# Transposed last 128 output columns: 72 matmuls of 512 columns in place of 288 of 128, in a gated attention and FFN kernel

## The chip, the cores and the metric

The kernel runs on one core of a Trainium2 chip. The metric is the device time of one execution in microseconds (us).

In the profile PE is TensorE, PEld its loads of the stationary operand ("weights"), DVE VectorE, ACT ScalarE and POOL GpSimd; SP issues transfers, which its queue (SPq) shows.

## The reference, cut to what matters

```python
# x: (1, 2048, 640) bf16; wqkv (640, 1920); wo (640, 640); w_gate, w_up (640, 1728); w_down (1728, 640)
g = sigmoid((x * gate_w).sum(-1, keepdims=True))     # one gate per row
a = linear_attention(x, wqkv, heads=32) @ wo         # (2048, 640)
b = (gelu(x @ w_gate) * (x @ w_up)) @ w_down         # (2048, 640)
return g * a + (1 - g) * b
```

Linear attention is reordered in the kernel so that its output is `pqn @ W2`, with `pqn` (2048 x 640) the normalised queries and `W2` (640 x 640) a small matrix made on the way.

## The kernel before: the parts that matter

One output row tile is 128 rows of 640 columns. The kernel's buffer in PSUM, where TensorE writes its results, is laid out as eight banks of 512 float32. 640 is more than one bank, so each product is made as one matmul of 512 columns and one of 128, both with the same stationary tile: `pqnT` for attention (FA, 5 chunks of the contraction) and `hT` for the FFN (FB, 13 chunks of 128 rows; the last 64 rows are the "half", done in pairs on the two halves of the array).

```python
def FA(i):                                       # attention part of row tile i
    for m in range(KC):                          # KC = 5
        lhs = pqnT[:, m, i * 128:(i + 1) * 128]
        e.matmul(ps[:, b0, :], lhs, w2[:, m, 0:512], ...)
        last = e.matmul(ps[:, b1, 0:128], lhs, w2[:, m, 512:640], ...)
    # ACT: t_sb[i] = g * result
# ... cut ...
def FB(i, main, tail, o):                        # FFN part of row tile i
    pieces = [(ps[:, main, :], 0, 512), (ps[:, tail, o:o + 128], 512, 128)]
    for fc in range(NFC - 1):                    # 13 chunks
        lhs = hT[fc][:, i * 128:(i + 1) * 128]
        for dst, c0, cn in pieces:
            last = e.matmul(dst, lhs, wd[:, fc, c0:c0 + cn], start=False, ...)
    # DVE, per piece: out = (1 - g) * result + t_sb[i]; SP: store.
    # For the very last tile, all 512-column matmuls come first, then its 128-column ones,
    # and each piece is mixed and stored by itself.
```

Earlier stages, whose matmuls are not changed: loads, K and Q projections, M = phi(K)^T x, then the FFN gate and up products with the GELU (71 to 191 us). Five DMA transposes of M feed the product "KV" inside the FFN stage. A row `z` of 640 float32 goes to DRAM, element by element, and comes back as a broadcast.

## Time and profile before

| | before |
|---|---|
| reported time, median of 6 fast runs | 275.88 us (275.61 to 276.31) |
| span of the profiled run | 274.5 us |
| TensorE (PE) busy; granted clock | 98%; 1.0 |
| first attention output matmul | 190.98 us |
| last matmul starts; end | 272.19 us; 274.48 us |

The page of the profile opens with the busy time of each engine (us, share of the span, number of instructions). Its part 4 is the chain of waits followed back from the last instruction.

```profile
span 274.5 us, 4041 instructions
PE 269.6 (98%) x1663; PEld 140.6 (51%) x1696; DVE 138.6 (50%) x234; ACT 78.5 (29%) x133; POOL 26.0 (9%) x28
...
PE 98%; issue 1%; DVE 0%
```

Almost the whole span is one chain of matmuls. The next lines are the timeline where the attention output stage begins: start in us, duration, engine, line, operation, shapes.

```profile
190.98 0.38 PE L754 MATMUL ps<-pool 128*128 128x512 bf16 x1
191.20 0.22 PE L755 MATMUL ps<-pool 128*128 128x128 bf16 x1
191.25 0.38 PE L754 MATMUL ps<-pool 128*128 128x512 bf16 x1
```

Durations overlap (0.38 us long, 0.22 us to the next start), so starts tell the cost. A 512-column matmul holds the stream for about 0.216 us and a 128-column one for about 0.056 us. The chain in order of time gives this more exactly: the two stretches below start 6.79 us apart and hold 25 pairs (a record is missing), 0.2716 us a pair.

```profile
213.69 6.74 PE ps L791 x49
220.48 6.74 PE ps L791 x49
```

The Trainium skill, "TensorE: Matmul & The Clock Gate", section "Wait — 56ns, not 53.3ns?", gives the same two figures, 215.7 and 55.6 ns, as the streamed columns at 2.4 GHz plus about 2.5 ns per matmul. This trace agrees.

Three more lines of the timeline mark instants that are compared later: the first Q matmul, the first FFN matmul and the last matmul.

```profile
8.75 0.38 PE L471 MATMUL ps<-pool 128*128 128x512 bf16 x1
71.36 0.81 PE L646 MATMUL ps<-pool 128*128 128x512 bf16 x3
272.19 0.22 PE L791 MATMUL ps<-pool 128*128 128x128 bf16 x1
```

These lines list the last mixes (DVE) and the last stores (issued by SP), with minimum, median and maximum duration in ns.

```profile
L802 DVE SCALAR_TENSOR_TENSOR pool<-ps,pool x2: 351/551/751, 271.7 to 272.4; 128x512 bf16<-128x512 f32 x1, 128x128 bf16<-128x128 f32 x1
L807 SPq DMA_DIRECT2D out_dram<-pool x2: 333/382/432, 272.5 to 272.9; - x2
```

The mix of 512 columns takes 751 ns. Its store is issued at 272.5 us and occupies SP for 333 ns, so the second and last store follows immediately behind it and takes 432 ns to issue.

### The profile page before, as it was taken

To read this page: it belongs to the slowest core of one execution; us is meant where nothing else is said; L and a number is where in the kernel's file an instruction comes from. 1 tells how busy PE (TensorE), PEld (TensorE's weight loads), DVE (VectorE), ACT (ScalarE), POOL (GpSimd) and SP (SyncE) were. 2 spreads that over 40 slices of the span, in tenths; PEclk is the share of its full clock that TensorE was granted. 3 is DMA by queue.
4 is the path that set the end of the run, shared out by engine and by line. 5 is a ranking of instruction groups with operands and counts; after the bars stand their busy time and mean duration, and the time that the engine had idled before them with its cause. 6 is when DMAs were issued, how large, how long until landed. Compare 5 with 4: busy or idle time off the path is not lost.

```text
span 274.5 us, 4041 instructions
## 1 busy us (share of the span) xinstructions
PE 269.6 (98%) x1663; PEld 140.6 (51%) x1696; DVE 138.6 (50%) x234; ACT 78.5 (29%) x133; POOL 26.0 (9%) x28
## 2 busy tenths in 40 slices
PE   8999999999999999999999999999999999999996
PEld 5555555555545444444444444444555555555553
DVE  1588888410234334999999998635000122212223
ACT  2455555210521453233222232224555100000000
POOL 5000000000000401242332421000000000000000
PEclk9999999999999999999999999999999999999999
DMA  7967999311120211112121121380000010111111
GB/s 226 176 109 121 367 405 380 89 23 27 24 48 22 51 49 50 39 32 48 26 49 33 39 50 25 73 297 14 0 0 2 23 43 32 48 50 48 50 42 54
DMA packets 37104, 22.54 MB, mean 82 GB/s; under 512 B 26463, under 2 KB 35679, under 8 KB 37087
## 3 DMA queue, kind: packets, MB, share of 16 engines
q1 hardware_dynamic: 36213, 21.31, 28.4%
q10 hardware_dynamic: 874, 0.98, 1.0%
q8 instruction: 13, 0.21, 0.3%
q14 instruction: 4, 0.03, 0.0%
HBM read 13.11 MB, written 2.62 MB: 57 GB/s over the span
## 4 chain that ended last, share of the span: by engine, by line
PE 98%; issue 1%; DVE 0%
PE ps L646 41%; PE ps L791 20%; PE ps L456 6%; PE ps L754 6%; PE ps L471 6%; PE ps L553 6%; PE ps L472 2%; PE ps L555 2%; PE ps L755 2%; PE ps L457 2%; PE ps L621 2%; PE ps L420 1%; PE ps L775 1%; PE ps L667 1%; PE ps L685 0%
## 5 line engine op out<-in xcount | busy, mean ns | idle before, releaser
L646 PE MATMUL ps<-pool 128*128 128x512 bf16 x509 | 113.0, 379 | 0.6
L646 PEld LDWEIGHTS ps<-pool 128*128 128x128 bf16 x520 | 50.4, 98 | 59.9
L791 PE MATMUL ps<-pool 128*128 128x128 bf16 (+1 forms) x407 | 56.6, 297 | 0.6 <-issue 0.2
L654 DVE TENSOR_TENSOR pool<-ps,pool 128x512 bf16<-128x512 f32 x52 | 35.7, 687 | 33.4 <-PE ps L646 30.2
L652 ACT ACTIVATE pool<-ps 128x512 f32<-128x512 f32 x52 | 31.0, 597 | 72.4 <-PE ps L646 72.0
L802 DVE SCALAR_TENSOR_TENSOR pool<-ps,pool 128x512 bf16<-128x512 f32 (+1 forms) x32 | 16.2, 547 | 63.8 <-PE ps L791 63.8
L791 PEld LDWEIGHTS ps<-pool 128*128 128x128 bf16 x416 | 31.9, 98 | 25.2 <-issue 1.1
L700 POOL TENSOR_TENSOR pool<-pool 128x640 f32<-128x640 bf16 x16 | 22.4, 1405 | 139.0 <-DMA pool<-z_row 86.5
L481 ACT ACTIVATE pool<-ps 128x640 bf16<-128x640 f32 x32 | 22.4, 704 | 24.0 <-PE ps L457 13.4
L495 DVE SCALAR_TENSOR_TENSOR pool<-ps,pool 128x640 bf16<-128x640 f32 x32 | 26.4, 824 | 2.2
L456 PE MATMUL ps<-pool 128*128 128x512 bf16 x78 | 23.6, 384 | 0.0
L708 DVE TENSOR_TENSOR pool<-pool 128x640 bf16<-128x640 bf16 x16 | 23.1, 1442 | 0.6
L471 PE MATMUL ps<-pool 128*128 128x512 bf16 x76 | 22.7, 379 | 0.1
L754 PE MATMUL ps<-pool 128*128 128x512 bf16 x77 | 21.3, 379 | 0.0
L553 PE MATMUL ps<-pool 128*128 128x512 bf16 x76 | 21.2, 379 | 0.0
L555 PE MATMUL ps<-pool 128*128 128x129 bf16 x80 | 17.6, 220 | 0.2
L472 PE MATMUL ps<-pool 128*128 128x129 bf16 x80 | 17.6, 220 | 0.2
L457 PE MATMUL ps<-pool 128*128 128x128 bf16 x80 | 17.6, 220 | 0.1
L755 PE MATMUL ps<-pool 128*128 128x128 bf16 x80 | 17.5, 219 | 0.2
L759 ACT ACTIVATE pool<-ps,pool 128x640 f32<-128x640 f32 x16 | 12.7, 794 | 9.2 <-PE ps L755 9.2
L491 DVE TENSOR_SCALAR pool<-pool 128x640 bf16<-128x640 bf16 x32 | 10.4, 326 | 5.4 <-ACT pool L481 4.2
L702 DVE TENSOR_REDUCE pool<-pool 128x32 f32<-128x640 f32 x16 | 12.9, 809 | 0.0
(52 smaller groups left out, 125.1 us busy)
## 6 DMA issues: line engine op xcount, KB each, us to landing
out_dram<-pool SPq DMA_DIRECT2D x15, 160.0 KB, 1.8
pool<-in_B_w_gate_dram SPq DMA_DIRECT2D x1, 2080.0 KB, 14.7
pool<-in_B_w_up_dram SPq DMA_DIRECT2D x1, 2080.0 KB, 19.4
pool<-in_A_x_dram SPq DMA_DIRECT2D x1, 1280.0 KB, 10.0
pool<-in_B_w_down_dram SPq DMA_DIRECT2D x1, 1120.0 KB, 5.9
pool<-in_A_x_dram SPq DMA_DIRECT2D x1, 960.0 KB, 5.9
pool<-in_A_wo_dram SPq DMA_DIRECT2D x6, 160.0 KB, 9.5
pool<-in_B_w_down_dram SPq DMA_DIRECT2D x1, 960.0 KB, 8.1
```

Of the source, the lines that this page charges most:

```text
L456: e.matmul(ps[:, b0, :], lhs, wk[:, k, 0:512], start=(k == 0), stop=(k == KC - 1))
L457: last = e.matmul(ps[:, b1, 0:128], lhs, wk[:, k, 512:640], start=(k == 0), stop=(k == KC - 1))
L471: e.matmul(ps[:, b0, :], lhs, wq[:, k, 0:512], start=(k == 0), stop=(k == KC - 1))
L472: last = e.matmul(ps[:, b1, 0:129], lhs, wq[:, k, 512:641], start=(k == 0), stop=(k == KC - 1))
L495: P.op("dve", lambda e: e.scalar_tensor_tensor(dst, ps_flat[:, b0 * 512:b0 * 512 + 640], 1.0 + EPS, e_buf[m], ALU.add, ALU.max), reads=[ba ...
L553: e.matmul(ps[:, bs[n], :], lhs, x_aug[:, i, 0:512], start=(i == 0), stop=(i == NT - 1))
L646: last = e.matmul(ps[:, b, :], w[:, k, fc * 128:(fc + 1) * 128], xT[:, k, j * 512:(j + 1) * 512], start=(k == 0), stop=(k == KC - 1))
L652: P.op("act", lambda e: e.activation(ge[n], ps[:, gb, :], ACT.Gelu_apprx_tanh), reads=[bank[gb]], writes=[r_ge[n]])
L654: P.op("dve", lambda e: e.tensor_tensor(hT[fc][:, j * 512:(j + 1) * 512], ps[:, ub, :], ge[n], ALU.mult), reads=[bank[ub], r_ge[n]], write ...
L708: P.op("dve", lambda e: e.tensor_tensor(pq[i].rearrange("p (h d) -> p h d", h=32), pq[i].rearrange("p (h d) -> p h d", h=32), den[n].unsqu ...
L754: e.matmul(ps[:, b0, :], lhs, w2[:, m, 0:512], start=(m == 0), stop=(m == KC - 1))
L791: last = e.matmul(dst, lhs, wd[:, fc, c0:c0 + cn], start=False, stop=(fc == NFC - 2), skip_group_check=True)
```

## The change

Columns 512 to 639 are now produced transposed: a 128-column slice of `W2` or `w_down` is the stationary tile and 512 rows of `pqnT` or `hT` are streamed past it. The intent is fewer and wider matmuls: 20 in place of 80 for attention, 52 in place of 208 for the FFN. In the transposed layout the gate differs along the free dimension, so the mix needs a broadcast row of 1 - g, which goes through DRAM; the result is turned back by a DMA transpose before it is stored. The half chunk is paired differently, PSUM banks are dealt out anew, and the last row tile is cut 384 + 128.

```diff
@@ (cut: addresses, views, resources; hT[13] half = j % 2 in place of alternate row tiles) @@
+            P.op("sp", lambda e: e.dma_start(omg_dram.rearrange("(i p) -> p i", p=128), omg,
+                                             allow_slow_non_contiguous=True),
+                 reads=[r_omg], writes=[r_od], dma=new_dma_key())
@@ (cut) @@
+                if g == 16:
+                    r_ob = P.sb("omgb", R_OB, R_OB + 2 * S)
+                    dma_in(omg_b, omg_dram.unsqueeze(0).broadcast_to([128, S]), [r_ob], reads=[r_od])
@@ (cut) FA @@
-                        e.matmul(ps[:, b0, :], lhs, w2[:, m, 0:512], start=(m == 0), stop=(m == KC - 1))
-                        last = e.matmul(ps[:, b1, 0:128], lhs, w2[:, m, 512:640],
+                        last = e.matmul(ps[:, b, :], pqnT[:, m, i * 128:(i + 1) * 128], w2[:, m, 0:512],
                                         start=(m == 0), stop=(m == KC - 1))
+            def FA_T(j):
+                    for m in range(KC):
+                        last = e.matmul(ps[:, b, :], w2[:, m, 512:640], pqnT[:, m, j * 512:(j + 1) * 512],
+                                        start=(m == 0), stop=(m == KC - 1))
@@ (cut) FFN @@
+            def FB_T(j, b):
+                    for fc in range(NFC - 1):
+                        last = e.matmul(ps[:, b, :], wd[:, fc, 512:640], hT[fc][:, j * 512:(j + 1) * 512],
+                                        start=False, stop=(fc == NFC - 2), skip_group_check=True)
+                P.op("dve", ... d = ps[:, b, :] - faT[j])
+                P.op("pool", ... d = d * omg_b[:, j * 512:(j + 1) * 512])
+                P.op("pool", ... outT[j] = d + faT[j])
+                P.op("sp", lambda e: e.dma_start_transpose(out_t[j], outT[j]), ...)
+                P.op("sp", ... store out_t[j] to out[0, j * 512:(j + 1) * 512, 512:640])
+            def FB(i, b, extra):
+                pieces = [(b, 0, 512)]
+                if i in extra:                                  # the last row tile
+                    pieces = [(b, 0, 384), (extra[i], 384, 512)]
+                # per piece: matmuls, mix on DVE, store
```

More of the change, by code (lines that the diff above doesn't have):

```diff
@@ L201, in bass_gated_mix__linear_attn_block__geglu_ffn__prompt_kernel @@
     R_T = R_WG
-    assert R_T + NT * 1280 <= R_MT + KC * 640
+    R_FT = R_T + NT * 1024
+    assert R_FT + NSC * 1024 <= R_MT + KC * 640
     R_WO = take(NHC * 640)
     R_W2C = take(NHC * 640)
+    R_OB = R_WO
+    assert R_OB + 2 * S <= R_W2C + NHC * 640
     R_W2 = take(KC * 640)
@@ L219, in bass_gated_mix__linear_attn_block__geglu_ffn__prompt_kernel @@
     TOTAL = off
+    omg_dram = nc.dram_tensor("omg_row", (S,), F32).ap()
     z_dram = nc.dram_tensor("z_row", (640,), F32).ap()
@@ L278, in bass_gated_mix__linear_attn_block__geglu_ffn__prompt_kernel @@
             hT = [v16(R_B + fc * S, S) for fc in range(NFC)]
-            t_sb = [v32(R_T + i * 1280, 640) for i in range(NT)]
-            out_sb = [v16(R_XT + i * 640, 640) for i in range(NT)]
+            t_sb = [v32(R_T + i * 1024, 512) for i in range(NT)]
+            faT = [v32(R_FT + j * 1024, 512) for j in range(NSC)]
+            omg_b = v32(R_OB, S)
+            out_sb = [v16(R_XT + i * 512, 512) for i in range(NT)]
+            outT = [v16(R_XT + NT * 512 + j * 512, 512) for j in range(NSC)]
+            out_t = [v16(R_WV + j * 512, 512).rearrange("p (t d) -> p t d", t=4) for j in range(NSC)]
             e_buf = [v16(R_E + n * 640, 640) for n in range(4)]
@@ L313, in bass_gated_mix__linear_attn_block__geglu_ffn__prompt_kernel @@
             r_mT = [P.sb("mT%d" % c, R_MT, R_MT + KC * 640) for c in range(KC)]
+            r_wo = [P.sb("wo%d" % c, R_WO + c * 640, R_WO + (c + 1) * 640) for c in range(NHC)]
+            r_w2c = [P.sb("w2c%d" % c, R_W2C + c * 640, R_W2C + (c + 1) * 640) for c in range(NHC)]
             r_e = [P.sb("e%d" % n, R_E + n * 640, R_E + (n + 1) * 640) for n in range(4)]
@@ L316, in bass_gated_mix__linear_attn_block__geglu_ffn__prompt_kernel @@
                 _r.fresh = False
-            r_wo = [P.res("wo%d" % c) for c in range(NHC)]
-            r_w2c = [P.res("w2c%d" % c) for c in range(NHC)]
             r_w2 = [P.res("w2_%d" % c) for c in range(NHC)]
@@ L326, in bass_gated_mix__linear_attn_block__geglu_ffn__prompt_kernel @@
             r_zd = P.res("z_dram")
+            r_od = P.res("omg_dram")
             r_den = [P.res("den%d" % n) for n in range(2)]
@@ L626, in G13 @@
                      reads=[bank[b]], writes=[r_ge[n]])
-                for h in range(2):
-                    def half(ap, h=h):
-                        return ap.rearrange("p (t two s) -> p t two s", two=2, s=128)[:, :, h, :]
-                    P.op("dve", lambda e, h=h, half=half: e.tensor_tensor(
-                        half(hT[fc][64 * h:64 * h + 64, j * 512:(j + 1) * 512]), half(ps[64:128, b, :]),
-                        half(ge[n][64:128, :]), ALU.mult),
-                        reads=[bank[b], r_ge[n]], writes=[r_hT[fc][j]])
+                h = j % 2
+                P.op("dve", lambda e: e.tensor_tensor(
+                    hT[fc][64 * h:64 * h + 64, j * 512:(j + 1) * 512], ps[64:128, b, :], ge[n][64:128, :], ALU.mult),
+                    reads=[bank[b], r_ge[n]], writes=[r_hT[fc][j]])
             def G(g):
@@ L734, in bass_gated_mix__linear_attn_block__geglu_ffn__prompt_kernel, with fa_bank @@
                 dma_in(wd[64 * h:64 * h + 64, 13, :], B_w_down[1664:1728, :], [r_wd13[h]])
-            r_t = [P.sb("t%d" % i, R_T + i * 1280, R_T + (i + 1) * 1280) for i in range(NT)]
-            r_out = [P.sb("out%d" % i, R_XT + i * 640, R_XT + (i + 1) * 640) for i in range(NT)]
+            r_t = [P.sb("t%d" % i, R_T + i * 1024, R_T + (i + 1) * 1024) for i in range(NT)]
+            r_fT = [P.sb("fT%d" % j, R_FT + j * 1024, R_FT + (j + 1) * 1024) for j in range(NSC)]
+            r_out = [P.sb("out%d" % i, R_XT + i * 512, R_XT + (i + 1) * 512) for i in range(NT)]
             r_out_b = [P.res("outb%d" % i) for i in range(NT)]
-            out_slot = [0]
-            def next_slot():
-                s = SLOTS[out_slot[0] % 4]
-                out_slot[0] += 1
-                return s
+            r_oT = [P.sb("oT%d" % j, R_XT + NT * 512 + j * 512, R_XT + NT * 512 + (j + 1) * 512)
+                    for j in range(NSC)]
+            r_ot = [P.sb("ot%d" % j, R_WV + j * 512, R_WV + (j + 1) * 512) for j in range(NSC)]
+            fa_ctr = [0]
+            def fa_bank():
+                b = fa_ctr[0] % 8
+                fa_ctr[0] += 1
+                return b
             def FA(i):
-                b0, b1 = next_slot()
+                b = fa_bank()
                 def fn(e):
@@ L752, in fn @@
                     for m in range(KC):
-                        lhs = pqnT[:, m, i * 128:(i + 1) * 128]
-                        e.matmul(ps[:, b0, :], lhs, w2[:, m, 0:512], start=(m == 0), stop=(m == KC - 1))
-                        last = e.matmul(ps[:, b1, 0:128], lhs, w2[:, m, 512:640],
+                        last = e.matmul(ps[:, b, :], pqnT[:, m, i * 128:(i + 1) * 128], w2[:, m, 0:512],
                                         start=(m == 0), stop=(m == KC - 1))
                     return last
-                P.op("pe", fn, reads=[r_pqT[i]] + r_w2, writes=[bank[b0], bank[b1]])
@@ L759, in FA @@
-                P.op("act", lambda e: e.activation(t_sb[i], ps_flat[:, b0 * 512:b0 * 512 + 640], ACT.Copy,
-                                                   scale=gg[:, i:i + 1]),
-                     reads=[bank[b0], bank[b1], r_g], writes=[r_t[i]])
-            def FB_half(i, main, tail):
+                P.op("pe", fn, reads=[r_pqT[i]] + r_w2, writes=[bank[b]])
+                P.op("act", lambda e: e.activation(t_sb[i], ps[:, b, :], ACT.Copy, scale=gg[:, i:i + 1]),
+                     reads=[bank[b], r_g], writes=[r_t[i]])
@@ L767, in fn @@
+            def FA_T(j):
+                b = fa_bank()
                 def fn(e):
                     last = None
-                    for p in range(2):
-                        for c0, cn in ((0, 512), (512, 128)):
-                            for h in range(2):
-                                t = 2 * p + h
-                                r = slice(64 * h, 64 * h + 64)
-                                dst = ps[:, main[t], :] if c0 == 0 else ps[:, tail[h], p * 128:p * 128 + 128]
-                                last = e.matmul(dst, hT[13][r, (i + t) * 128:(i + t + 1) * 128],
-                                                wd[r, 13, c0:c0 + cn], start=(c0 == 0 or p == 0), stop=False,
-                                                skip_group_check=True)
@@ L778, in fn @@
-                    return last
-                P.op("pe", fn, reads=[r_hT[13][i // 4]] + r_wd13, writes=[bank[b] for b in main + tail])
-            def FB(i, main, tail, o):
-                rd = [r_hT[fc][i // 4] for fc in range(NFC - 1)] + r_wd
-                pieces = [(ps[:, main, :], 0, 512), (ps[:, tail, o:o + 128], 512, 128)]
-                def mk(ps_):
-                    def fn(e):
+                    for m in range(KC):
+                        last = e.matmul(ps[:, b, :], w2[:, m, 512:640], pqnT[:, m, j * 512:(j + 1) * 512],
+                                        start=(m == 0), stop=(m == KC - 1))
@@ new lines, in fn, with FB_half @@
+                    return last
+                P.op("pe", fn, reads=r_pqT[4 * j:4 * j + 4] + r_w2, writes=[bank[b]])
+                P.op("act", lambda e: e.activation(faT[j], ps[:, b, :], ACT.Copy),
+                     reads=[bank[b]], writes=[r_fT[j]])
+            def FB_half(j, us, main, tail, extra):
+                def fn(e):
+                    last = None
+                    for u in us:
+                        for h in range(2):
+                            i = 4 * (j + h) + u
+                            r = slice(64 * h, 64 * h + 64)
+                            cuts = [(main[i], 0, 512)]
+                            if i in extra:
+                                cuts = [(main[i], 0, 384), (extra[i], 384, 512)]
+                            for b, c0, c1 in cuts:
+                                last = e.matmul(ps[:, b, 0:c1 - c0], hT[13][r, i * 128:(i + 1) * 128],
+                                                wd[r, 13, c0:c1], start=True, stop=False, skip_group_check=True)
+                    if tail:
+                        for h in range(2):
+                            r = slice(64 * h, 64 * h + 64)
+                            last = e.matmul(ps[:, tail[h], :], wd[r, 13, 512:640],
+                                            hT[13][r, (j + h) * 512:(j + h + 1) * 512],
+                                            start=True, stop=False, skip_group_check=True)
+                    return last
+                P.op("pe", fn, reads=[r_hT[13][j], r_hT[13][j + 1]] + r_wd13,
+                     writes=[bank[main[4 * (j + h) + u]] for u in us for h in range(2)] +
+                     [bank[b] for b in tail] + [bank[b] for b in extra.values()])
@@ new lines, in FB_T, with fn @@
+            def FB_T(j, b):
+                n = j % 2
+                def fn(e):
+                    last = None
+                    for fc in range(NFC - 1):
+                        last = e.matmul(ps[:, b, :], wd[:, fc, 512:640], hT[fc][:, j * 512:(j + 1) * 512],
+                                        start=False, stop=(fc == NFC - 2), skip_group_check=True)
+                    return last
+                P.op("pe", fn, reads=[r_hT[fc][j] for fc in range(NFC - 1)] + r_wd, writes=[bank[b]])
+                d = tmp[n][:, 0:512]
+                P.op("dve", lambda e: e.tensor_tensor(d, ps[:, b, :], faT[j], ALU.subtract),
+                     reads=[bank[b], r_fT[j]], writes=[r_tmp[n]])
+                P.op("pool", lambda e: e.tensor_tensor(d, d, omg_b[:, j * 512:(j + 1) * 512], ALU.mult),
+                     reads=[r_tmp[n], r_ob], writes=[r_tmp[n]])
+                P.op("pool", lambda e: e.tensor_tensor(outT[j], d, faT[j], ALU.add),
+                     reads=[r_tmp[n], r_fT[j]], writes=[r_oT[j]])
+                P.op("sp", lambda e: e.dma_start_transpose(out_t[j], outT[j]),
+                     reads=[r_oT[j]], writes=[r_ot[j]], dma=new_dma_key())
+                P.op("sp", lambda e: e.dma_start(
+                    out[0, j * 512:(j + 1) * 512, 512:640].rearrange("(t p) d -> p t d", p=128), out_t[j]),
+                    reads=[r_ot[j]], dma="out")
@@ L787, in fn @@
+            def FB(i, b, extra):
+                rd = [r_hT[fc][i // 4] for fc in range(NFC - 1)] + r_wd
+                pieces = [(b, 0, 512)]
+                if i in extra:
+                    pieces = [(b, 0, 384), (extra[i], 384, 512)]
+                for n, (pb, c0, c1) in enumerate(pieces):
+                    def fn(e, pb=pb, c0=c0, c1=c1):
                         last = None
                         for fc in range(NFC - 1):
-                            lhs = hT[fc][:, i * 128:(i + 1) * 128]
@@ L790, in fn @@
-                            for dst, c0, cn in ps_:
-                                last = e.matmul(dst, lhs, wd[:, fc, c0:c0 + cn], start=False,
-                                                stop=(fc == NFC - 2), skip_group_check=True)
-                        return last
-                    return fn
-                end = i == NT - 1
-                if not end:
-                    P.op("pe", mk(pieces), reads=rd, writes=[bank[main], bank[tail]])
-                for n, (src, c0, cn) in enumerate(pieces):
-                    b = (main, tail)[n]
-                    if end:
-                        P.op("pe", mk([pieces[n]]), reads=rd, writes=[bank[b]])
-                    P.op("dve", lambda e, src=src, c0=c0, cn=cn: e.scalar_tensor_tensor(
-                        out_sb[i][:, c0:c0 + cn], src, omg[:, i:i + 1], t_sb[i][:, c0:c0 + cn],
-                        ALU.mult, ALU.add),
-                        reads=[bank[b], r_t[i], r_omg], writes=[r_out[i] if n == 0 else r_out_b[i]])
-                    if end:
-                        P.op("sp", lambda e, c0=c0, cn=cn: e.dma_start(
-                            out[0, i * 128:(i + 1) * 128, c0:c0 + cn], out_sb[i][:, c0:c0 + cn]),
-                            reads=[r_out[i] if n == 0 else r_out_b[i]], dma="out")
@@ L810, in FB @@
-                if not end:
-                    P.op("sp", lambda e: e.dma_start(out[0, i * 128:(i + 1) * 128, :], out_sb[i]),
-                         reads=[r_out[i], r_out_b[i]], dma="out")
-            for i in range(NT):
-                FA(i)
-            free = [0, 1, 2, 3, 4, 5, 6, 7]
-            for i in range(0, NT, 4):
-                main, tail = free[0:4], free[4:6]
-                FB_half(i, main, tail)
-                for t in range(4):
-                    FB(i + t, main[t], tail[t % 2], (t // 2) * 128)
-                free = free[6:8] + [main[0], main[1], main[2], tail[0], main[3], tail[1]]
+                            last = e.matmul(ps[:, pb, 0:c1 - c0], hT[fc][:, i * 128:(i + 1) * 128],
+                                            wd[:, fc, c0:c1], start=False, stop=(fc == NFC - 2),
+                                            skip_group_check=True)
@@ new lines, in fn @@
+                        return last
+                    r = (r_out, r_out_b)[n][i]
+                    P.op("pe", fn, reads=rd, writes=[bank[pb]])
+                    P.op("dve", lambda e, pb=pb, c0=c0, c1=c1: e.scalar_tensor_tensor(
+                        out_sb[i][:, c0:c1], ps[:, pb, 0:c1 - c0], omg[:, i:i + 1], t_sb[i][:, c0:c1],
+                        ALU.mult, ALU.add),
+                        reads=[bank[pb], r_t[i], r_omg], writes=[r])
+                    P.op("sp", lambda e, c0=c0, c1=c1: e.dma_start(
+                        out[0, i * 128:(i + 1) * 128, c0:c1], out_sb[i][:, c0:c1]), reads=[r], dma="out")
@@ new lines, in bass_gated_mix__linear_attn_block__geglu_ffn__prompt_kernel @@
+            for j in range(NSC):
+                for i in range(4 * j, 4 * j + 4):
+                    FA(i)
+                FA_T(j)
+            for s_, (m1, tail, m2) in enumerate((((4, 5, 6, 7), (0, 1), (2, 3, 0, 1)),
+                                                 ((4, 5, 6, 7), (2, 3), (0, 1, 2, 3)))):
+                j = 2 * s_
+                for us, ms in (((0, 1), m1), ((2, 3), m2)):
+                    order = [4 * (j + h) + u for u in us for h in range(2)]
+                    main = dict(zip(order, ms))
+                    extra = {NT - 1: 4} if NT - 1 in order else {}
+                    FB_half(j, us, main, tail if us[0] == 0 else (), extra)
+                    if us[0] == 0:
+                        FB_T(j, tail[0])
+                        FB_T(j + 1, tail[1])
+                    for i in order:
+                        FB(i, main[i], extra)
```

## The prediction

> **What bounds the kernel.** TensorE. The page gives PE 98% busy at granted clock 1.0, and the chain of waits is PE for 98% of the 274.5 us span. DVE is at 50%, ACT 29%, POOL 9%. So only what shortens or stalls the matmul stream changes the time.
>
> **What the stream costs now.** In the timeline, 512-column matmuls back to back start every 0.216 us (ten of the FFN group take 2.16). In the output stage a 512 and a 128 column matmul share one stationary tile; 25 such pairs start over 6.79 us (213.69 to 220.48), 0.2716 a pair, so a 128-column one costs 0.0558 us. The weight loads (98 ns each in the groups) are hidden already: no idle time stands at them inside the runs of pairs. The Trainium skill, "TensorE: Matmul & The Clock Gate", section "Wait — 56ns, not 53.3ns?", gives 55.6 and 215.7 ns, with about 2.5 ns fixed per matmul; this trace agrees.
>
> **What the change does on PE.** Columns 512-639 need the same streamed columns either way: attention 80 and FFN 208 matmuls of 128 become 20 and 52 of 512. 288 x 0.0558 = 16.07 us become 72 x 0.2158 = 15.54 us. The gain is 216 fixed costs of 2.5 ns, 0.53 us. The 64-row half chunk (half calls) keeps its paired row halves: 8 pairs of 512 and 8 of 128 become 10 pairs of 512 (the last tile is cut 384 + 128), the same within 0.05 us. Its four entries and exits (two "issue" gaps of about 0.27 us each) remain four. Fewer weight loads free nothing.
>
> **Off the critical path.** ACT: four more copies, each shorter (0.6 us against 0.79), one per 1.08 us of PE. DVE: the mixes lose their 128-wide pieces and gain four subtracts (about 0.69 us). POOL: eight 128x512 operations, about 1.2 us each, estimated from 1.405 us for 128x640. Four DMA transposes (2.6 us to landing) and stores follow; the last some 25 us before the end. Output buffers are not reused, so late stores hold up nobody. The end (128-column piece, mix, 1.6 us store) stays.
>
> **The one real risk.** The gate row goes to DRAM as 2048 four-byte elements, issued at about 52 us on the queue that then carries the five transposes of M (issued 59.8 to 76.9). The similar row of 640 elements took 10.6 us to land. Taking 2 us as fixed, 13.5 ns an element, so 2048 take about 28 us and land at 82 to 84 us. The Trainium skill, "DMA: Bandwidth & Descriptors", section on HWDGE ordering, says that a semaphore increment lands only after every earlier write of that DMA engine; so the transposes may be reported done only then, and PE needs them at 84.5 us (the KV product). No run yet shows it. Probably it just fits; if the transposes move only after the row, PE stalls 1 to 4 us there.
>
> **Prediction.** 275.5 us, range 274.9 to 278.5. Chances: faster by over 2% 0.01, within 2% 0.94, slower by over 2% 0.05.
>
> **What the profile would show.** Attention output stage 20 groups of 1.08 us, about 21.6 us against 21.7; FFN output stage shorter by about 0.4 us; PE still about 98%. The weight-load count falls by 216. The row's landing time is 20 to 35 us; the KV product starts at 84.5 us, or later by the stall.
>
> **What would make it wrong.** The tiny-element write taking over 35 us, or blocking the queue (slower); transposed-output matmuls not running at 0.216 us; a bank wait at the switch of stages; or a hidden weight-load limit in the pairs that I don't see (faster, but by little).

## More of the kernel before

A profile of one execution goes with each kernel; its span is about 1.3 us shorter than the reported time in most executions (1.7 in a few, the profiled one of the kernel before among them: 276.21 us reported, span 274.48).

Runs "in one look" are single executions without a verdict; only their traces are used.

## The result, and the profile after

| | before | after |
|---|---|---|
| reported time, median of 6 fast runs | 275.88 us | 274.82 us (274.61 to 274.97) |
| ratio of fast runs, 95% interval | | 0.9959 (0.9946 to 0.9972) |
| span of the profiled run | 274.476 us | 273.577 us |

A ratio is the mean time of one kernel's fast runs over that of the other's fast runs of the same rounds, so it is not quite the ratio of the medians. The kernel is 0.4% faster, but the gain is 1.06 us by the medians where 0.4 us was predicted (0.53 us less an allowance for a stall), and 274.82 us lies just under the range.

```profile
span 273.6 us, 3628 instructions
PE 269.2 (98%) x1454; PEld 131.4 (48%) x1482; DVE 136.8 (50%) x219; ACT 79.2 (29%) x137; POOL 36.2 (13%) x36
...
PE 96%; DMA 2%; issue 1%; SPq 0%; DVE 0%
```

Weight loads fell by 214. That is exact, counted in the two kernels: 216 fewer in the transposed products, 11 fewer in the half chunk, 13 more because the last tile is cut 384 + 128, which the prediction's sum left out. PE records fell by 209, because some are missing. POOL took on 10 us of work; SP waited for it before the transposes, no matmul did. The 2% of DMA in the chain is a load at the start. The next lines are from the chain in order of time. A transposed attention group (L784) of five matmuls takes 1.08 us, 0.216 us a matmul.

```profile
195.25 1.08 PE ps L784 x5
200.64 1.08 PE ps L784 x5
```

The four instants of the changed kernel are these lines of its timeline: first Q matmul, first FFN matmul, first attention output matmul, last matmul.

```profile
8.53 0.38 PE L481 MATMUL ps<-pool 128*128 128x512 bf16 x1
71.15 1.03 PE L656 MATMUL ps<-pool 128*128 128x512 bf16 x4
190.77 0.81 PE L771 MATMUL ps<-pool 128*128 128x512 bf16 x3
271.45 0.22 PE L849 MATMUL ps<-pool 128*128 128x128 bf16 x1
```

At the end (views of the two source lines of the changed kernel, durations in ns as above) the store before the last is issued earlier (271.6 us, behind a mix of 384 columns that takes 618 ns), and the last store takes 350 ns to issue in place of 432.

```profile
L855 DVE SCALAR_TENSOR_TENSOR pool<-ps,pool x2: 351/484/618, 271.0 to 271.7; 128x384 bf16<-128x384 f32 x1, 128x128 bf16<-128x128 f32 x1
L859 SPq DMA_DIRECT2D out_dram<-pool x2: 333/342/350, 271.6 to 272.1; - x2
```

The single records of the two traces place the difference of the spans, 0.899 us, completely:

| stretch | before | after | gain |
|---|---|---|---|
| start to the first FFN matmul | 71.363 | 71.148 | 0.215 |
| to the first attention output matmul | 119.618 | 119.618 | 0.000 |
| attention output, to the first half chunk | 21.829 | 21.679 | 0.150 |
| FFN output, to the start of the last matmul | 59.380 | 59.007 | 0.373 |
| start of the last matmul to the end | 2.286 | 2.125 | 0.161 |

The two matmul stretches together gain 0.523 us, as the sum of the prediction had it. What it did not have is 0.161 us at the end and 0.215 us at the start. The start's difference is there by the first Q matmul (8.749 against 8.532 us), where the code is the same. The gate row, feared to take 28 us, landed in 10.8. These lines from the list of DMA issues of the changed kernel give a transfer, its size in KB and its time from issue to landing in us.

```profile
omg_row<-pool SPq DMA_DIRECT2D x1, 8.0 KB, 10.8
z_row<-pool SPq DMA_DIRECT2D x1, 2.5 KB, 8.3
```

### The profile page after: what moved, and what is told of

It reads as the page before. It is cut to its first block, busy times and chain, and to the rows that moved or that the text cites. A ratio compares the mean times of both kernels' runs of the same rounds, so it can differ in the third digit from the quotient of the medians.

```text
span 273.6 us, 3628 instructions
## 1 busy us (share of the span) xinstructions
PE 269.2 (98%) x1454; PEld 131.4 (48%) x1482; DVE 136.8 (50%) x219; ACT 79.2 (29%) x137; POOL 36.2 (13%) x36
## 4 chain that ended last, share of the span: by engine, by line
PE 96%; DMA 2%; issue 1%; SPq 0%; DVE 0%
PE ps L656 41%; PE ps L849 16%; PE ps L771 6%; PE ps L481 6%; PE ps L566 6%; PE ps L466 6%; PE ps L823 4%; PE ps L568 2%; PE ps L482 2%; PE ps L467 2%; DMA pool<-in_A_wqkv_dram 2%; PE ps L634 2%; PE ps L784 2%; PE ps L804 1%; PE ps L677 1%
## 5 line engine op out<-in xcount | busy, mean ns | idle before, releaser
L656 PE MATMUL ps<-pool 128*128 128x512 bf16 x509 | 113.0, 379 | 0.6
L656 PEld LDWEIGHTS ps<-pool 128*128 128x128 bf16 x520 | 50.4, 98 | 59.9
L849 PE MATMUL ps<-pool 128*128 128x512 bf16 (+2 forms) x218 | 45.4, 366 | 0.2
L849 PEld LDWEIGHTS ps<-pool 128*128 128x128 bf16 x221 | 21.0, 98 | 24.3 <-issue 0.6
L491 ACT ACTIVATE pool<-ps 128x640 bf16<-128x640 f32 x32 | 22.4, 704 | 23.8 <-PE ps L467 13.4
L855 DVE SCALAR_TENSOR_TENSOR pool<-ps,pool 128x512 bf16<-128x512 f32 (+2 forms) x17 | 12.2, 719 | 33.7 <-PE ps L849 33.6
L466 PE MATMUL ps<-pool 128*128 128x512 bf16 x78 | 23.7, 383 | 0.1
L481 PE MATMUL ps<-pool 128*128 128x512 bf16 x76 | 22.7, 379 | 0.0
L566 PE MATMUL ps<-pool 128*128 128x512 bf16 x76 | 21.2, 379 | 0.0
L828 DVE TENSOR_TENSOR pool<-ps,pool 128x512 f32<-128x512 f32 x4 | 2.8, 692 | 31.0 <-remote 23.9
L771 PE MATMUL ps<-pool 128*128 128x512 bf16 x78 | 17.8, 379 | 0.1
L467 PE MATMUL ps<-pool 128*128 128x128 bf16 x80 | 17.6, 220 | 0.1
L830 POOL TENSOR_TENSOR pool<-pool 128x512 f32<-128x512 f32 x4 | 5.1, 1266 | 75.7 <-DVE pool L828 75.7
L501 DVE TENSOR_SCALAR pool<-pool 128x640 bf16<-128x640 bf16 x32 | 10.4, 326 | 5.2 <-ACT pool L491 3.9
```

The source lines that it names most:

```text
L466: e.matmul(ps[:, b0, :], lhs, wk[:, k, 0:512], start=(k == 0), stop=(k == KC - 1))
L467: last = e.matmul(ps[:, b1, 0:128], lhs, wk[:, k, 512:640], start=(k == 0), stop=(k == KC - 1))
L481: e.matmul(ps[:, b0, :], lhs, wq[:, k, 0:512], start=(k == 0), stop=(k == KC - 1))
L566: e.matmul(ps[:, bs[n], :], lhs, x_aug[:, i, 0:512], start=(i == 0), stop=(i == NT - 1))
L656: last = e.matmul(ps[:, b, :], w[:, k, fc * 128:(fc + 1) * 128], xT[:, k, j * 512:(j + 1) * 512], start=(k == 0), stop=(k == KC - 1))
L771: last = e.matmul(ps[:, b, :], pqnT[:, m, i * 128:(i + 1) * 128], w2[:, m, 0:512], start=(m == 0), stop=(m == KC - 1))
```

## The experiments

Theory: the matmul count is worth 0.52 us, the new end of the kernel another 0.15 us, and the remainder is the scatter of single executions. Rivals: the count is worth more than 2.5 ns a matmul (hidden weight loads), or something systematic in the changed program shortens the start.

In every run the times between the first FFN matmul and the first attention output matmul came out at 119.617 to 119.619 us, so stretches of the trace can be compared to a few ns although reported times scatter by several tenths of a us. From the first Q matmul to the first FFN matmul it was 62.613 to 62.617 us in all 13 profiles, so what differs in the start arises in the first 9.5 us.

### A second look at the kernel before

No edit.

> The kernel before, unchanged, as a second look at it. Only the fixed cost of the matmuls (theory M: 216 fewer at about 2.5 ns, 0.53 us) was predicted to matter, while 1.06 us was measured and 0.90 us stands in the two profiles: 0.52 us in the output stage, 0.215 us before the first FFN matmul (71.363 against 71.148 us) and 0.161 us after the last matmul (2.286 against 2.125 us). Rival N (scatter of single executions): this profile's start of the FFN stage lies anywhere between 71.1 and 71.4 us, its end 2.1 to 2.3 us. Rival S (something systematic, such as the shorter program or the cut of the last tile): the same 71.36 and 2.29 us come again, within 0.05 us. Ratio to before 1.000 +- 0.001 under all.

Measured: 275.68 us, ratio 0.9992 (0.9967 to 1.0017). The first FFN matmul starts at 71.329 us, the matmul stretch is 81.209 us as before, the end 2.279 us (2.286 before). The line below, from the view of one source line, shows its last two stores: minimum, median and maximum duration in ns.

```profile
L807 SPq DMA_DIRECT2D out_dram<-pool x2: 333/382/432, 272.5 to 272.8; - x2
```

The end is systematic: the same 333 and 432 ns came again. The start came again too here, but other runs below moved it by up to 0.94 us. Single executions of this unchanged kernel ranged from 275.22 to 276.26 us, with one more at 277.7 that widened the intervals: 1 us, as large as the gain under study.

### The matmuls cut back to 128 columns

```diff
-    last = e.matmul(ps[:, b, :], w2[:, m, 512:640], pqnT[:, m, j * 512:(j + 1) * 512], ...)
+    for q in range(0, 512, 128):
+        last = e.matmul(ps[:, b, q:q + 128], w2[:, m, 512:640],
+                        pqnT[:, m, j * 512 + q:j * 512 + q + 128], ...)
```

The same was done in the FFN product; everything else is the changed kernel.

> The changed kernel with the transposed products again in matmuls of 128 columns (288 in place of 72, the same streamed columns), all else as changed: the reverse dose of theory M. M expects the stretch from the first attention output matmul to the last matmul, 80.686 us after and 81.209 before, at 81.2 us, the time at 275.3 to 275.4 us, and no idle PE, since a 98 ns weight load per 128 columns was hidden before as well. If the whole 1.06 us came from the matmuls and their weight loads, the time goes to 275.9 us. If the change gained from something else than the number of matmuls, the stretch stays at 80.7 us.

Measured: 275.52 us, ratio to before 0.9985 (0.9963 to 1.0008). Three lines of this run's timeline follow. The first is where the attention output begins and the second shows a transposed group in pieces, 13 starts in 0.67 us (0.89 less the 0.22 of the last one); the third is the last matmul.

```profile
190.86 0.81 PE L771 MATMUL ps<-pool 128*128 128x512 bf16 x3
195.18 0.89 PE L785 MATMUL ps<-pool 128*128 128x128 bf16 x13
272.09 0.22 PE L853 MATMUL ps<-pool 128*128 128x128 bf16 x1
```

The stretch is 272.089 - 190.864 = 81.225 us. It had been 81.209 before and 80.686 after: putting 216 matmuls back costs 0.539 us, 2.5 ns each, and nothing else in the stretch changed. The theory of the count holds, and its rival, a further gain from weight loads saved, falls.

### The matmuls cut to 64 columns

The same edit with 64 in place of 128.

> The changed kernel with the transposed products in matmuls of 64 columns (576 in place of 72). Where does the prediction's 'hidden weight load' end? If only the streamed columns and about 2.5 ns a matmul count, the stretch from the first attention output matmul to the last matmul grows by 504 x 2.5 ns = 1.3 us, to 81.9 us. If a weight load of 128 columns takes as long as some 55 ns of streaming and is exposed as soon as a matmul is shorter, each 64-column one takes about 56 ns, 576 take 32 us in place of 15.5, and the stretch is about 97 us.

Measured in one look: 276.38 us; the stretch is 273.001 - 191.056 = 81.945 us, 1.259 us more than after, exactly 504 x 2.5 ns. In the line below from this run's timeline, 19 matmuls of 64 columns start within 0.53 us (0.72 less 0.19), 29 ns apart.

```profile
195.37 0.72 PE L785 MATMUL ps<-pool 128*128 128x64 bf16 x19
```

The view of that source line shows that each of the 160 attention matmuls had a weight load of its own, 98 ns long:

```profile
L785 PEld LDWEIGHTS ps<-pool x160: 97/98/98, 195.2 to 212.9; 128*128 128x128 bf16 x160
```

Even here the loads are hidden: their records are 98 ns long but, like the matmuls, start 29 ns apart, and loads saved gain nothing. Eight loads in a row bring the same tile here, so this run alone does not show it for a new tile each time. The run with the cut 448 + 64 below does: its last 13 matmuls, of 64 columns, have a tile each, and the 12 loads in this line of that run's timeline start within 0.32 us (0.42 less 0.10), again 29 ns apart.

```profile
271.56 0.42 PEld L849 LDWEIGHTS ps<-pool 128*128 128x128 bf16 x12
```

### The kernel before with the new end (first attempt)

```diff
-    pieces = [(ps[:, main, :], 0, 512), (ps[:, tail, o:o + 128], 512, 128)]
+    pieces = [(ps[:, tail, o:o + 128], 512, 128), (ps[:, main, 0:384], 0, 384),
+              (ps[:, ex, 0:128], 384, 128)]      # last tile only; ex = free[6]
@@ (cut: the same pieces in the half chunk; banks, results and stores per piece) @@
```

> The kernel before with only the end of the changed one: the last tile in pieces of 128, 384 and 128 columns, mixed and stored one by one, so that the last two are as in the changed kernel. Theory E (the end got shorter because the store before the last one is issued earlier, behind a 384-column mix, and is smaller): from the last matmul's start to the end 2.13 us as after, not 2.29 us; the time 275.7 to 275.8 us. Rival N (scatter): the end is anywhere from 2.1 to 2.3 us, as in the second look at before.

Measured: 276.48 us, ratio 1.002 (0.9998 to 1.0042). The experiment had a mistake: `free[6]` was a bank whose last result was still being read. PE waited 0.85 us for DVE at the last half chunk, as the bracket at the end of this line of its timeline says:

```profile
258.39 0.72 PE L779 MATMUL ps<-pool 64*128 64x512 bf16 x9 [0.85 <-DVE pool L813]
```

Its end, though, measured 2.145 us, as theory E had it. The miss also shows what one wrongly chosen bank costs: more than the whole change gains on the matmuls.

### The kernel before with the new end (mended)

```diff
-              (ps[:, ex, 0:128], 384, 128)]      # ex = free[6]
+              (ps[:, ex, 256:384], 384, 128)]    # ex = the tile's own second bank, unused columns
@@ (cut: the same in the half chunk) @@
```

> e4 without its mistake: the extra piece of the last tile had been given a bank still being read, and PE waited 0.85 us for DVE. Now it goes into unused columns of the last tile's second bank. Theory E: from the last matmul's start to the end 2.14 us (before: 2.28 and 2.29), the matmul stretch of the output stage as before, 81.21 us plus 0.03 to 0.1 us for the extra matmuls, and no wait of PE for DVE; the time about 0.1 us under before's, less than the rounds can show, so the profile decides.

Measured: 275.61 us, ratio 0.9993 (0.9978 to 1.0008). The matmul stretch is 81.245 us (0.036 more, as expected), and the end 2.130 us. The last two stores now issue in 332 and 347 ns, as the view of their source line shows:

```profile
L819 SPq DMA_DIRECT2D out_dram<-pool x2: 332/340/347, 272.2 to 272.7; - x2
```

So the cut of the last tile alone, transplanted into the old kernel, accounts for the shorter end: 0.15 us. In the traces of the first comparison it is made up so: the last store is issued 0.08 us after its mix ended before and 0.03 after, its issue is 0.08 us shorter, and the rest of its way to landing 0.03 us shorter. The reported times cannot resolve that; the stretches can.

### The changed kernel without the cut

```diff
-                    extra = {NT - 1: 4} if NT - 1 in order else {}
+                    extra = {}
```

> The changed kernel without the cut of the last tile: one piece of 512 columns is mixed and stored after the last matmul. All theories: the end grows by the longer mix (0.73 against 0.35 us) and by a larger last store, 2.5 to 2.6 us against 2.125; the matmul stretch is 0.03 us shorter; the time 275.1 to 275.3 us. So the change as written owes about 0.4 us of its gain to keeping a 128-column piece at the end, as before had.

Measured: 275.7 us, ratio 0.9993 (0.9969 to 1.0017). The end is 2.933 us, longer than expected; the last matmul starts 0.194 us sooner (stretch 80.492), because it is a longer one. The lines are the last two matmuls, the mix and the store.

```profile
271.98 0.59 PE L849 MATMUL ps<-pool 128*128 128x512 bf16 x2
272.61 0.75 DVE L855 SCALAR_TENSOR_TENSOR pool<-ps,pool 128x512 bf16<-128x512 f32 x1 [2.05 <-PE ps L849]
273.39 0.33 SPq L859 DMA_DIRECT2D out_dram<-pool  x1
```

The net loss against the changed kernel is 0.614 us: without the cut, the end would have given back nearly all that the transposed matmuls gain. Stretch and end together are 83.425 us, against 83.495 before and 82.811 after, which leaves 0.07 us. In this run the first FFN matmul started at 72.085 us, because the Q projection waited 0.99 us for its weights (a line of its timeline):

```profile
9.47 0.38 PE L481 MATMUL ps<-pool 128*128 128x512 bf16 x1 [0.99 <-DMA pool<-in_A_wqkv_dram]
```

In this run, then, the scatter of the start is a matter of when the first weights land.

### The last tile cut 448 + 64

```diff
-    pieces = [(b, 0, 384), (extra[i], 384, 512)]
+    pieces = [(b, 0, 448), (extra[i], 448, 512)]
```

> The changed kernel with the last tile cut 448 + 64 in place of 384 + 128, an attempt at a better end. The 64-column mix is shorter by 64 elements of a row (about 0.07 us at 1 ns an element) and the last matmul by 0.027 us, so the end is about 2.03 us after the last matmul starts, against 2.125. If 64-column matmuls run at their streaming rate, the matmul stretch is unchanged and the whole gains 0.09 us; if they are held at some 56 ns by weight loads, the stretch grows by 13 x 27 ns = 0.35 us and it loses 0.25 us. Time 274.7 to 275.1 us; the profile decides.

Measured: 275.67 us, ratio to before 0.9996 (0.9982 to 1.001). The attempt to better the end failed. The 64-column matmuls cost no extra (stretch 80.713), but the end grew to 2.511 us. The last product now takes so little time that its mix waits for the mix of 448 columns (682 ns), and the last store is again issued right behind another and takes 437 ns. It is this store that sets the end: the last mix had ended at 272.64 us, the store ahead held SP until 272.81, and the last store began at 272.85. These two lines, for mix and store, are those of the views of their source lines in this run:

```profile
L855 DVE SCALAR_TENSOR_TENSOR pool<-ps,pool x2: 273/478/682, 271.8 to 272.4; 128x448 bf16<-128x448 f32 x1, 128x64 bf16<-128x64 f32 x1
L859 SPq DMA_DIRECT2D out_dram<-pool x2: 332/384/437, 272.5 to 272.8; - x2
```

The last piece has to be long enough to cover the mix and the store issue of the piece ahead of it. 384 + 128 was the best of the cuts tried.

### The changed kernel again, twice

No edit.

> The changed kernel, unchanged, again. Known by now: 0.54 us from the matmul count (e2) and 0.14 to 0.16 us from the end (e4) make 0.69 us; 1.06 us was measured. The last 0.37 us came before the first FFN matmul, where the profiles so far give 71.15 us for the changed kernel and 71.25, 71.33, 71.36, 71.38 and 72.09 for others with the same code there. Theory N (scatter of the loads at the start): now 0.5 to 0.9 us faster than before (ratio 0.9967 to 0.9982), single runs spread over some 0.7 us as before's do, and a start drawn anew. Rival S (the changed program itself starts faster): ratio 0.996 again and 71.1 us to the first FFN matmul.

> The changed kernel a third time, for the 0.2 to 0.3 us that remain. Accounted for so far by profiles that repeat to a few ns: 0.523 us (matmul stretch, 81.209 to 80.686), 0.15 us (end), and about 0.07 us between the span and the reported time (1.25 against 1.32 us). Sum 0.74 us, ratio 0.9973. Theory N (the rest is the draw of the start): ratio 0.9965 to 0.9985 now. Rival S (the changed program starts earlier by 0.25 us): 0.996 a third time. Pooled over three calls a difference of 0.1 us can be told.

Measured: 274.88 us, ratio 0.9964 (0.9946 to 0.9981), and later 275.06 us, ratio 0.9972 (0.9959 to 0.9985). In their profiles the matmul stretch is 80.686 and 80.687 us and the end 2.131 and 2.132 us, while the first FFN matmul starts at 71.778 and 71.441 us. So everything after the start repeats within 7 ns, and the start does not: with the first profile the changed kernel drew 71.15, 71.44 and 71.78 us, the kernel before 71.33 and 71.36 us. The early start of the first comparison was a draw.

The record allows a wider check, because it gives the span of nearly every execution. If what follows the first FFN matmul takes as long in each as in the profile of its kernel, the rest of a span is its start. The start comes to 71.36 us on average in 37 executions of the changed kernel and its edited forms, and to 71.38 us in 48 of the kernel before and its edited forms; the difference of 0.02 us has a standard error of 0.08 us. So no earlier start of the changed program shows. The changed kernel itself drew 71.09, 71.29 and 71.32 us on average in its three looks. The ratios went from 0.9959 over 0.9964 to 0.9972, whereas the accounted sum is 0.9973.

### How small writes land

Six writes to scratch DRAM were added to the changed kernel at a time when the SP queue was idle, one after the other. (Only behind the last, `pr_f`, was something else issued while it was under way: a DMA transpose, 0.4 us later.)

```diff
+            probe(pr_a.rearrange("(i p) -> p i", p=128), 1)      # 128 elements of 4 bytes
+            probe(pr_b.rearrange("(p i) -> p i", p=128), 16)     # 128 runs of 64 bytes
+            probe(pr_c.rearrange("(i p) -> p i", p=128), 5)      # as the z row
+            probe(pr_d.rearrange("(i p) -> p i", p=128), 16)     # as the gate row
+            # pr_e: 2048 elements, 64 bytes apart
+            probe(pr_f.rearrange("(i p) -> p i", p=128), 32)
```

> The changed kernel with six writes to scratch DRAM added on the SP queue, each after the one before has landed, after the last weight load: a, 128 elements of 4 bytes; b, 128 runs of 64 bytes; c, 640 elements as the z row; d, 2048 elements as the gate row; e, 2048 elements each in a 64-byte line of its own; f, 4096 elements. The prediction's step (13.5 ns an element): a 3.7, c 10.6, d 29, e 29, f 57 us to landing. Rival L (16 elements share a 64-byte line and their writes follow one another, lines in parallel): a, c, d and f all 8 to 11 us, e and b 2 to 3 us. Rival F (a fixed cost of some 7 us and a few ns an element): a 7, c 8, d 11, e 11, f 15 us. Result unchanged; the time grows only if the late stores reach the end.

Measured in one look (275.28 us, result correct). The lines are from the list of DMA issues, with the time from issue to landing in us at the end:

```profile
pr_a<-pool SPq DMA_DIRECT2D x1, 0.5 KB, 7.6
pr_b<-pool SPq DMA_DIRECT2D x1, 8.0 KB, 1.4
pr_c<-pool SPq DMA_DIRECT2D x1, 2.5 KB, 8.2
pr_d<-pool SPq DMA_DIRECT2D x1, 8.0 KB, 11.9
pr_e<-pool SPq DMA_DIRECT2D x1, 8.0 KB, 4.4
pr_f<-pool SPq DMA_DIRECT2D x1, 16.0 KB, 16.4
```

None of the three models holds alone. The prediction's 13.5 ns an element is out: from 128 to 4096 elements the time grows by 8.8 us, 2.2 ns an element. A fixed cost of small writes (rival F) is out too, because 2048 elements 64 bytes apart take 4.4 us and not 11.9. What the small ones share is that elements next to each other in DRAM are written as separate 4-byte pieces (the packet count of the page grows by 9184, for 8960 elements and 128 runs): the same 2048 elements land 7.5 us sooner when they are spread out, and 128 packed ones take longer than 2048 spread ones. That packed pieces hold each other up is the plain reading; by what mechanism, and whether 64 bytes is the unit that matters, was not tested. Rival L expected this floor but not the growth with the count.

### The gate row written late

The write at 52 us is removed (not shown) and made here:

```diff
                 if g == 1:       # ahead of the last three transposes of M
+                    P.op("sp", lambda e: e.dma_start(omg_dram.rearrange("(i p) -> p i", p=128), omg, ...),
+                         reads=[r_omg, r_z5[1]], writes=[r_od], dma=new_dma_key())
```

> The changed kernel with the write of the gate row moved from 52 to about 72 us, ahead of the last three transposes of M, which land at 75 to 78 us otherwise. Theory O (a completion is counted only after the earlier writes of the same DMA engines): all three land with or after the row, at 83 us or later, and the KV product, due at 84.1 us, begins on time or up to 3 us late. Rival I (independent completion): they land at 75 to 78 us and nothing moves.

Measured in one look (275.57 us): the row was issued at 72.29 us and landed 10.4 us later, at 82.7. Two lines of the SP queue's timeline show it and the three transposes issued behind it:

```profile
72.29 0.37 SPq L590 DMA_DIRECT2D omg_row<-pool  x1
73.53 3.85 SPq L594 DMA_TRANSPOSE pool<-pool  x3
```

The view of the transposes' source line gives the landing of all five (two had been issued before the row):

```profile
DMA to landing us min/median/max: 2.6/7.7/9.6
```

In the changed kernel the five take 2.6 to 3.8 us; the 3.8 is the first, issued at 59.6 us and landed at 63.4, with the row landing at 63.1. So the transposes behind the row were reported only after it: the records of this trace have them landing at 83.14, 83.61 and 83.78 us. In the run with the probes the transpose issued 0.4 us behind `pr_f` took 16.8 us to landing where 2.4 is usual, and it too landed after the write ahead of it (238.6 and 237.8 us). The late report that the prediction feared is real and agrees with the Trainium skill, "DMA: Bandwidth & Descriptors", section "Queues, rings and completion order": a semaphore increment lands only after the earlier writes of that engine. The KV product still began 12.95 us after the first FFN matmul, as in the changed kernel, so it cost nothing. Whether the data of the transposes arrived late, or only the report of it, is not shown. For the z row, issued next at 77.43 us, it was more than the report: it landed 8.1 us after the gate row (13.4 us after its issue, 8.3 in the changed kernel), the time that such a row takes alone, which suggests that the two rows did not overlap.

## Why the prediction was right or wrong

- **PE bounds the kernel, and only its stream counts: right.** The stretch between loads and output stage did not move by more than 1 ns, whatever else was changed.
- **0.53 us for 216 matmuls fewer: right.** It measured 0.523 us, and putting the matmuls back cost 0.539 us. (With the 13 that the cut of the last tile adds, 203 fewer outside the half chunk make 0.51 us.) The parts were also right: attention 0.150 (0.15 predicted), FFN 0.373 (0.4 predicted).
- **Weight loads are hidden: right**, even at 64 columns.
- **ACT, DVE, POOL and the transposes off the path: right.** POOL took 1.27 us per operation (1.2 predicted), a transpose 2.4 us to landing.
- **"The end (128-column piece, mix, 1.6 us store) stays": wrong.** This is the step of the mechanism that failed; the allowance in the next point is the other. The last piece stays, but the piece before it shrank from 512 to 384 columns, so its mix is done sooner (618 against 751 ns), its store is off SP before the last one is due, and the last store issues in 350 in place of 432 ns. Transplanting the cut moved 2.28 us to 2.13 us, 0.15 us. I had read the end as a sum of its last three steps and not asked what the step before them still occupied.
- **"13.5 ns an element, so 2048 take about 28 us": wrong.** The row took 10.8 us. From this I allowed for a stall, which moved the forecast up by about 0.15 us; no matmul waited for the transposes or the row. One point (640 elements, 10.6 us) and an assumed fixed cost of 2 us cannot give a slope; the probes give 2.2 ns an element from 128 to 4096. Nor was the point a fixed one: the same z row took 10.2 to 10.8 us in the four profiles of the kernel before and its edited forms, and 8.1 to 9.3 in those of the changed kernel that leave the gate row at its place; why is open.
- **The range was too narrow below.** Its lower end, 274.9 us, lay 0.5 us under the matmul gain's own estimate, 275.4, and single executions of an unchanged kernel scatter by 1 us.
- **The rest was luck.** The forecast of 275.5 lies 0.68 us above the measured 274.82. The end (0.15 us), the allowance (0.15) and the last item of the sum below (0.06) make about half. The remainder is about the size of the draw of the start in that first comparison, 71.09 us on average where all looks together give 71.36.

The sum now: 0.523 (matmuls) + 0.153 (end, the mean of two looks before and of three after) + about 0.06 us between the span and the reported time (1.32 us in the runs of the second look at before, 1.26 us in 16 runs of the changed kernel; its cause is open) = 0.74 us, ratio 0.9973. Measured: 0.9959, 0.9964 and 0.9972. Each interval either includes 0.9973 or misses it by a hair (0.9972 is the upper end of the first). Some 0.2 us of the mean of the three stays unaccounted. The changed kernel's 16 executions drew a start of 71.22 us on average, those of the kernel before (37 with a known span) 71.42, which is as much. That the difference is chance rests on the check above, in which edited forms with the same start are counted in and no difference is left; it excludes an effect of 0.2 us with little to spare (standard error 0.08).

## What to carry to other kernels

In a stream that is PE-bound with loads hidden, swapping the operands so that a narrow remainder becomes wide saves about 2.5 ns for every matmul that vanishes and nothing for the weight loads; multiply this out before taking on layouts, broadcasts and transposes for it. The end of a kernel deserves its own sum, with the previous piece's mix and store in it: the choice of the last cut (none, 384 + 128, 448 + 64) moved up to 0.6 us here, more than the 216 matmuls. Where a gain is smaller than the scatter of whole executions, compare stretches of the trace between two fixed instructions, which repeat to a few ns.

## What the Trainium skill lacked or had wrong

- "TensorE: Matmul & The Clock Gate", section "Back-to-back issue gap", states a sustained 81 ns a matmul for 128 columns and 131 ns for 512 with weight loads between them. With one load per matmul, the runs show 55.8 and 215.8 ns, and 29 ns for 64 columns; the section's plain formula, which it gives for isolated matmuls, fits all three, the sustained figures neither of theirs.
- The same page, section "LDWEIGHTS (loading the stationary operand)", gives a load's time by its columns (107 ns for 128 by its formula; 98 ns in these records). That section does not say how narrow a matmul can be before such a load shows in the stream: with a load for each 64-column matmul, every 29 ns, the loads still cost nothing.
- "DMA: Bandwidth & Descriptors" has no figure for rows of 4-byte elements written to DRAM from 128 partitions: 7.6 us for 128 elements, 11.9 for 2048, 16.4 for 4096, against 4.4 for 2048 elements placed 64 bytes apart and 1.4 for 128 runs of 64 bytes. Its fixed cost of about 2 us (section "Anatomy of one DMA — SWDGE (gpsimd) path", for transfers issued from GpSimd, while these were issued from SP) does not cover this.
- I found on no page that a store issued from SP right behind another takes longer to issue: 432 and 437 ns with 0.04 us between them, against 347 to 350 ns with 0.13 us, and mostly 332 or 333 ns where SP had been idle for over 1.5 us.
